# A fused attention and gated-MLP kernel: in block 0, tile 1 turned in two halves around a step of V's first pass, the first half of tile 0's copy cut in two, and tile 2's norm moved behind tile 1's copies

## Chip, cores, metric

One core of one Trainium2 chip. The metric is device time in microseconds (us): the median of several executions. One execution of each kernel is also recorded by the hardware profiler; its span is usually about 1.7 us shorter than the device time (up to about 3 us in single runs). Times like 10.47 below are microseconds from the start of that span.

## The reference, cut

Two rounds of attention (local, dilated, 32 heads) and a gated MLP, each behind a norm, on x of 2048 rows and 1024 columns in bf16:

```python
x = A_x
x = x + _A_ref(_layernorm(x), A_wqkv, A_wo)           # 8 keys per query, 2 apart
x = x + _B_ref(_layernorm(x), W_gate, W_up, W_down)   # relu(gate) * up, then down
# ... the same two lines once more
```

Only the very first step matters here: `_layernorm(x)` of the first 512 rows (block 0, four tiles of 128 rows) and the product of the result with V's weights.

## The kernel before

The opening normalizes tiles 0 to 3, turns each on TensorE (eight 128x128 transposes into PSUM, where TensorE leaves its results), and copies the turned tile to SBUF in two halves. V's first pass is the consumer: for tile 0, four "steps" kc = 0..3 of eight products each, one per chunk of output columns. Step kc reads one eighth of the turned tile and one eighth of the weights. The weights of these steps come in two transfers: rows kc 0 and 1, then rows kc 2 and 3.

```python
def turn(t):
    if t == 0:      # two PSUM tiles, one per half
        tps[t] = [psum.tile([P, KC // 2, P], BF16, tag="acc", name=f"tp{h}")[:] for h in range(2)]
    else:           # one PSUM tile of two banks; each half in a bank of its own
        both = psum_l.tile([P, 2, KC, P], BF16, tag="L", name="tp_pair")
        tps[t] = [both[:, h, 0:KC // 2, :] for h in range(2)]
    for c in range(KC):
        ...         # eight transposes, in order on TensorE

def copy(t, eng, h):
    f = nc.vector.tensor_copy if eng == "v" else nc.scalar.copy
    on(eng, f, hold["xnT"][:, t, h * (KC // 2):(h + 1) * (KC // 2), :], tps[t][h])

scratch(13)                        # 13 products on ones, to warm TensorE up
bn(0, 0); bn(0, 1); aggr(0)        # VectorE: statistics of tile 0
act_square(2); act_mean(2)         # ScalarE: statistics of tile 2
bn(1, 0); apply(0, 0); apply(0, 1)
turn(0); copy(0, "a", 0)           # ScalarE copies the first half of tile 0
bn(1, 1); aggr(1)
copy(0, "v", 1)
act_power(2)
apply(1, 0); apply(1, 1)           # norm of tile 1, in halves, on VectorE

def second():
    turn(1)
    apply(2)                       # norm of tile 2, on VectorE
    copy(1, "v", 0); copy(1, "v", 1)
    act_square(3); act_mean(3); act_power(3); apply(3)
# ... and in V's first pass:
for kc in range(KC // 2):          # KC = 8: four steps for tile 0
    if kc == KC // 2 - 1:
        ln["second"]()             # tile 1 is turned before the fourth step
    for c in range(KC):
        prod(kc, c, 0, 1)
# next on TensorE: 32 products of tile 1, which read the first half of its copy
```

The several instructions of one engine are issued in the order written. Waits between engines are put in by the language, from the tiles that the instructions read and write.

## Time and profile before

| | before |
|---|---|
| device time, median of 3 runs | 1618.47 us (1617.82 to 1618.52) |
| span of the profiled run | 1616.7 us |
| TensorE busy | 1611.1 us |
| first product of V, tile 0 | 7.89 us |
| first product of V, tile 1 | 10.47 us |

Busy times and clock, from the page of the kernel before (busy us, share of the span, instructions; PEclk is the granted clock in tenths, 9 for full, in 40 slices):

```profile
span 1616.7 us, 18929 instructions
PE 1611.1 (100%) x7633; PEld 786.4 (49%) x7633; DVE 1137.4 (70%) x960; ACT 475.5 (29%) x967; POOL 180.9 (11%) x168
PEclk9999999999999999999999999999999999999999
```

TensorE is busy but for 5.6 us, so an edit that leaves its work as it is can gain only where TensorE stands still. The waits of PE, then those of its weight loads for transfers, of the kernel before (total us, times, longest):

```profile
PE scratch L132 <- DVE ones L310: 1.5, 1, 1.5
PE acc_v L132 <- ACT xnT_first L328: 0.6, 1, 0.6
PE acc_v L132 <- DVE xnT_first L106: 0.2, 1, 0.2
```

```profile
PEld L132 <- DMA w_u<-in_B_W_up_dram: 0.6, 1, 0.6
PEld L132 <- DMA w_o<-in_A_wo_dram: 0.5, 1, 0.5
PEld L132 <- DMA w_v<-in_A_wqkv_dram: 0.3, 1, 0.3
```

The first product of V waits 0.6 us for ScalarE's copy, the first product of tile 1 0.2 us for VectorE's. These two waits are what the change is after. The timeline of the kernel before around them (start, duration, engine, line, instruction, then in brackets the engine's idle time and who ended it):

```profile
7.27 0.56 ACT L328 COPY xnT_first<-tp 128x512 bf16<-128x512 bf16 x1
...
7.89 1.51 PE L132 MATMUL acc_v<-xnT_first,w_v 128*128 128x128 bf16 x24 [0.60 <-ACT xnT_first L328]
...
8.63 0.74 DVE L106 TENSOR_SCALAR xn_first<-x,mv,rstd 128x512 bf16<-128x512 bf16 x2 [0.54 <-POOL rstd L328]
...
9.23 0.61 PE L383 MATMUL tp_pair<-ident,xn_first 128*128 128x128 bf16 x8
...
9.54 0.55 DVE L106 TENSOR_SCALAR xn_first<-x,mean,rstd 128x1024 bf16<-128x1024 bf16 x1 [0.17 <-POOL rstd L328]
...
9.68 0.61 PE L132 MATMUL acc_v<-xnT_first,w_v 128*128 128x128 bf16 x8
10.00 0.75 DVE L106 COPY xnT_first<-tp_pair 128x512 bf16<-128x512 bf16 x2
...
10.47 0.72 PE L132 MATMUL acc_v<-xnT_first,w_v 128*128 128x128 bf16 x10 [0.18 <-DVE xnT_first L106]
```

Read it so: 24 products (steps kc 0 to 2), eight transposes of tile 1 (`tp_pair`), the fourth step (9.68), then the products of tile 1 (10.47). VectorE applies tile 2's norm at 9.54, and tile 1's copies follow at 10.00.

### The profile page before, as it was taken

What the parts mean: (1) busy time and instruction counts of PE and PEld (TensorE: products, weight loads), DVE (VectorE), ACT (ScalarE), POOL (GpSimd) and SP (SyncE); (2) the same over time, 40 slices, a digit from 0 to 9 for tenths busy, and PEclk for the clock granted to TensorE, in tenths of its full rate; (3) what the DMA queues carried; (4) which work ended last, traced back from release to release, by engine and by line L of the source; (5) the groups of instructions that cost most, each with busy time, mean ns of one, the idle gap of its engine ahead of it and who ended that gap; (6) DMA issues with size and microseconds to landing.
All of it is one profiled execution on the core that took longest, in us unless ns stands there. A gap on an engine that the chain in (4) does not pass through costs nothing.

```text
span 1616.7 us, 18929 instructions
## 1 busy us (share of the span) xinstructions
PE 1611.1 (100%) x7633; PEld 786.4 (49%) x7633; DVE 1137.4 (70%) x960; ACT 475.5 (29%) x967; POOL 180.9 (11%) x168
## 2 busy tenths in 40 slices
PE   9999999999999999999999999999999999999999
PEld 6646544444444445444454444544445444444444
DVE  5999979996989698929489293893939939311211
ACT  5753312131116313603136031360313311131110
POOL 2400100010003002300053000530005100000000
PEclk9999999999999999999999999999999999999999
DMA  9868868697669766794747947479574884755452
GB/s 302 186 187 242 222 158 261 183 215 204 209 190 220 199 183 213 191 247 149 223 159 204 239 152 228 154 202 256 160 230 153 209 240 156 209 161 177 157 167 67
DMA packets 407448, 317.92 MB, mean 197 GB/s; under 512 B 166464, under 2 KB 387008, under 8 KB 406848
## 3 DMA queue, kind: packets, MB, share of 16 engines
q1 hardware_dynamic: 406784, 316.13, 69.5%
q8 instruction: 59, 0.97, 0.2%
q10 hardware_dynamic: 576, 0.59, 0.1%
q14 instruction: 29, 0.24, 0.0%
HBM read 266.29 MB, written 34.66 MB: 186 GB/s over the span
## 4 chain that ended last, share of the span: by engine, by line
PE 99%; DMA 1%; DVE 0%; POOL 0%; issue 0%; DVEq 0%
PE acc_u L132 24%; PE acc_g L132 24%; PE dacc L132 18%; PE acc_wo L132 7%; PE acc_q L132 7%; PE acc_k L132 7%; PE acc_v L132 7%; PE dacc_pair L132 6%; DMA w_u<-in_B_W_up_dram 0%; DMA x<-in_A_x_dram 0%; POOL rstd L328 0%; DVE xn_first L106 0%; DVE bst L106 0%; PE tp_pair L383 0%; DVE bst L103 0%
## 5 line engine op out<-in xcount | busy, mean ns | idle before, releaser
L132 PE MATMUL acc_u<-xnT_b,w_u 128*128 128x512 bf16 x1792 | 423.3, 379 | 0.1
L132 PE MATMUL acc_g<-xnT_b,w_g 128*128 128x512 bf16 x1792 | 423.3, 379 | 0.0
L784 ACT ACTIVATE r<-acc_g 128x512 bf16<-128x512 f32 x224 | 133.6, 596 | 725.4 <-PE acc_g L132 699.4
L106 DVE TENSOR_TENSOR hT<-acc_u,r 128x512 bf16<-128x512 f32 x224 | 151.3, 690 | 240.6 <-PE acc_u L132 238.2
L132 PE MATMUL dacc<-w_d,hT 128*128 128x512 bf16 (+1 forms) x1400 | 301.9, 375 | 0.0
L132 PEld LDWEIGHTS <-hT 128*128 128x128 bf16 x1820 | 178.1, 98 | 209.0
L132 PEld LDWEIGHTS <-w_u 128*128 128x128 bf16 x1792 | 175.3, 98 | 211.7 <-DMA w_u<-in_B_W_up_dram 0.6
L132 PEld LDWEIGHTS <-w_g 128*128 128x128 bf16 x1792 | 175.3, 98 | 211.4
L106 DVE TENSOR_TENSOR pv<-a,vhm 128x4096 bf16<-128x4096 bf16 x64 | 143.7, 2290 | 0.0
L831 DVE TENSOR_TENSOR x<-dacc,x 128x512 bf16<-128x512 f32 (+1 forms) x38 | 24.5, 673 | 154.1 <-PE dacc L132 154.1
L602 DVE TENSOR_TENSOR t<-q,k 128x2048 f32<-128x2048 bf16 x56 | 128.1, 2293 | 6.7 <-ACT k L537 4.6
L106 DVE TENSOR_TENSOR t<-q,k 128x2048 f32<-128x2048 bf16 x56 | 127.6, 2290 | 3.7 <-ACT k L537 2.6
L106 DVE TENSOR_TENSOR pv<-pv 128x1024 bf16<-128x1024 bf16 (+1 forms) x128 | 113.9, 957 | 0.0
L543 POOL COPY kh<-k 128x14 bf16<-128x14 bf16 x40 | 56.0, 1405 | 504.4 <-ACT k L537 504.4
L132 PE MATMUL acc_wo<-w_o,oT 128*128 128x512 bf16 x512 | 112.0, 379 | 0.0
L615 DVE TENSOR_TENSOR ac<-ac,t 128x2048 f32<-128x2048 f32 x48 | 109.7, 2286 | 0.3
L106 DVE TENSOR_TENSOR ac<-ac,t 128x2048 f32<-128x2048 f32 x48 | 109.8, 2288 | 0.0
L264 POOL TENSOR_TENSOR st_b<-st_b,neg_half 128x1 f32<-128x1 f32 x29 | 43.9, 1521 | 526.2 <-ACT st_b L263 526.2
L132 PE MATMUL dacc_pair<-w_d,hT 128*128 128x512 bf16 x420 | 95.9, 379 | 0.0
L132 PEld LDWEIGHTS <-oT 128*128 128x128 bf16 x512 | 50.1, 98 | 60.6 <-DMA w_o<-in_A_wo_dram 0.5
L259 ACT ACTIVATE xn_b<-x 128x1024 bf16<-128x1024 bf16 x29 | 30.3, 1045 | 128.4 <-DVE x L106 66.3
L441 ACT CAST vT<-acc_v 128x512 bf16<-128x512 f32 x56 | 32.7, 586 | 57.7 <-PE acc_v L132 56.7
(134 smaller groups left out, 1230.1 us busy)
## 6 DMA issues: line engine op xcount, KB each, us to landing
w_g<-in_B_W_gate_dram SPq DMA_DIRECT2D x56, 1024.0 KB, 7.2
w_u<-in_B_W_up_dram SPq DMA_DIRECT2D x56, 1024.0 KB, 5.3
w_d<-in_B_W_down_dram SPq DMA_DIRECT2D x48, 1024.0 KB, 5.7
w_o<-in_A_wo_dram SPq DMA_DIRECT2D x16, 1024.0 KB, 7.1
vhm<-v_d SPq DMA_DIRECT2D x32, 284.0 KB, 6.8
v_d<-vT SPq DMA_DIRECT2D x8, 1024.0 KB, 9.6
oT<-o_d SPq DMA_DIRECT2D x32, 256.0 KB, 4.0
w_d<-in_B_W_down_dram SPq DMA_DIRECT2D x16, 512.0 KB, 3.8
```

What stands on the lines that cost most here:

```text
L106: tail_dve[0] = f(*args, **kwargs).ins
L132: tail_pe[0] = nc.tensor.matmul(*args, **kwargs).ins
L259: nc.scalar.activation(xn, xt[:], ACT.Square, accum_out=sq)
L264: nc.gpsimd.tensor_tensor(rstd, vpe, neg_half[:, 0:1], op=ALU.pow)
L441: tail_act[0] = nc.scalar.copy(st["vT"][:, c, :], acc[:]).ins
L543: nc.gpsimd.tensor_copy(khalo[n][:, c, :], k[:, BLK:BLK + HALO])
L602: nc.vector.tensor_tensor(t[:], i0, i1, op=ALU.mult)
L615: nc.vector.tensor_tensor(o, ac[:], t[:], op=ALU.add)
L784: tail_act[0] = nc.scalar.activation(rs[j][:], acc[:], ACT.Relu).ins
L831: run = dv if n < NB - 2 else (lambda f, *args, **kwargs: f(*args, **kwargs))
```

## The change

The intent: let V start when a quarter of tile 0 is copied (ScalarE's half is copied in two quarters, VectorE's half stays whole); turn only the first half of tile 1 before the fourth step, so that its copy runs under that step; and let tile 1's copies go ahead of tile 2's norm on VectorE.

```diff
-        def turn(t):
-            if t == 0:
+        def turn(t, halves=(0, 1)):
+            if t in tps:
+                pass
+            elif t == 0:
 ...
-            for c in range(KC):
+            for c in (h * (KC // 2) + i for h in halves for i in range(KC // 2)):
 ...
-        def copy(t, eng, h):
+        def copy(t, eng, h, i0=0, i1=KC // 2):
 ...
-        copy(0, "a", 0)
+        copy(0, "a", 0, 0, KC // 4)
+        copy(0, "a", 0, KC // 4, KC // 2)
 ...
-        def second():
-            turn(1)
+        def second(h):
+            turn(1, (h,))
+            if h == 0:
+                copy(1, "v", 0)
+                return
+            copy(1, "v", 1)
             apply(2)
-            copy(1, "v", 0)
-            copy(1, "v", 1)
             act_square(3)
 ...
                 if kc == KC // 2 - 1:
-                    ln["second"]()
+                    ln["second"](0)
                 for c in range(KC):
                     prod(kc, c, 0, 1)
+            ln["second"](1)
```

More of the change, by code (lines that the diff above doesn't have):

```diff
@@ L384, in turn @@
                                                      xna[:, t, c * P:(c + 1) * P], ident[:]).ins
-        def copy(t, eng, h):
+        def copy(t, eng, h, i0=0, i1=KC // 2):
             f = nc.vector.tensor_copy if eng == "v" else nc.scalar.copy
-            on(eng, f, hold["xnT"][:, t, h * (KC // 2):(h + 1) * (KC // 2), :], tps[t][h])
+            on(eng, f, hold["xnT"][:, t, h * (KC // 2) + i0:h * (KC // 2) + i1, :], tps[t][h][:, i0:i1, :])
         warm = small("warm")
```

## The prediction

> **What bounds the kernel now.** TensorE: busy 1611.1 of 1616.7 us (the page's busy times), 99% of the chain of waits, clock 1.0. After the opening 10.5 us only two weight loads wait visibly (w_u 0.6 us, w_o 0.5 us). So the change can win only in the opening, where the waits of PE list 0.60 us at 7.89 (first product waits for ScalarE's copy of tile 0) and 0.18 us at 10.47 (first product of tile 1 waits for VectorE's copy; 0.34 us of issue time).
>
> **The three parts, read from the timeline.**
> 1. *Quartered copy.* ScalarE takes 1.057 us for 1024 columns and 0.565 for 512, so I estimate 0.32 for 256: the first products could start at about 7.64, not 7.89. But the third step's weights are the second w_v transfer, which lands at 8.73; its weight load starts at 8.774 already now. Sixteen products at 56 ns (the Trainium skill, "TensorE: Matmul & The Clock Gate", section "Wait — 56ns, not 53.3ns?", gives the same 56) end at 8.53 and then wait about 0.25 us for that DMA. The wait only moves; worth about 0.
> 2. *Norm of tile 2 later.* Its 0.55 us on VectorE (9.54 to 10.09) now delays tile 1's first copy (10.00). Moved, it costs nothing: its reader, the turn of tile 2, starts at 14.0.
> 3. *Tile 1 in halves.* Four transposes at 9.23, step 4 from 9.46 to 9.90, four more transposes. The first copy can start at about 9.67 and end at 10.08. PE's work is contiguous to 10.13, so tile 1's products could start then: 0.34 us earlier. However both halves share one PSUM tile, and the trace shows dependencies kept for whole tiles: ScalarE's copy of tile 3 waits for all eight transposes (17.735), VectorE's copy of the other half waits for ScalarE's (18.353), the additions of dacc_pair wait for both halves (708.77). The Trainium skill, "PSUM — Partial Sum Buffer", section "PSUM bank collisions raise a hardware error", says different banks run clean, so this is the program's own caution. If it also holds writer after reader, the last four transposes wait for the copy (about 10.13), end at 10.36, and the gain is only 0.11 us. I think this more likely.
>
> **On the critical path.** 0.1 to 0.35 us in all, carried to the end because later DMA issues follow PE's releases; w_v's last rows (landed 12.107, wanted 12.474) leave room. The added ScalarE copy (0.3 us) falls on an engine idle until 9.43. The spread of the three runs is 0.7 us, larger than the gain.
>
> **Predicted:** 1618.3 us, 8 in 10 between 1617.4 and 1619.0. Faster by over 2%: 0.003; within 2%: 0.994; slower: 0.003.
>
> **What would show each step.** Right: first w_v product near 7.64; a new wait for w_v of about 0.25 us ending near 8.77; VectorE's tile-1 copy near 9.67; PE waiting 0.2 us for that copy before the second four transposes, or no wait (then 0.34 us gained); first tile-1 product at 10.13 to 10.36; everything later shifted by that amount. Wrong: the third step starts before 8.7, or tile 1's products start at 10.47 or later.
>
> **What would make it wrong.** The w_v transfer landing earlier (then part 1 counts, up to 0.25 us); the split turn making PE wait longer; an instruction order changed far from the edit, moving the two later DMA waits; drift between runs larger than the effect.

## The result

| | before | after |
|---|---|---|
| device time, median of 5 runs | 1618.47 us (1617.82 to 1618.78) | 1618.19 us (1618.10 to 1618.90) |
| span of the profiled run | 1616.7 us | 1616.4 us |
| second half of x tile 0 landed | 3.78 | 4.20 |
| second w_v transfer landed | 8.73 | 8.11 |
| first product of V, tile 0 | 7.89 | 8.09 |
| first product of V, tile 1 | 10.47 | 10.64 |

The ratio of after to before is 0.9999, with a 95% interval of 0.9986 to 1.0013: the same. (A ratio is the mean time of one kernel's fast runs over the mean of the other's fast runs of the same rounds, so it is not quite the ratio of the medians.)

The same lines of the kernel after: busy times, waits of PE (its weight loads now wait for no transfer at all), timeline:

```profile
span 1616.4 us, 18930 instructions
PE 1611.3 (100%) x7633; PEld 786.6 (49%) x7633; DVE 1137.1 (70%) x960; ACT 475.8 (29%) x968; POOL 180.4 (11%) x168
```

```profile
PE scratch L132 <- DVE ones L310: 1.5, 1, 1.5
PE acc_v L132 <- ACT xnT_first L328: 0.4, 1, 0.4
```

```profile
7.68 0.63 ACT L328 COPY xnT_first<-tp 128x256 bf16<-128x256 bf16 x2
...
8.09 1.50 PE L132 MATMUL acc_v<-xnT_first,w_v 128*128 128x128 bf16 x24 [0.40 <-ACT xnT_first L328]
...
9.04 0.74 DVE L106 TENSOR_SCALAR xn_first<-x,mv,rstd 128x512 bf16<-128x512 bf16 x2 [0.54 <-POOL rstd L328]
...
9.51 0.40 PE L385 MATMUL tp_pair<-ident,xn_first 128*128 128x128 bf16 x4
...
9.74 0.61 PE L132 MATMUL acc_v<-xnT_first,w_v 128*128 128x128 bf16 x8
...
9.94 0.42 DVE L106 COPY xnT_first<-tp_pair 128x512 bf16<-128x512 bf16 x1 [0.17 <-PE tp_pair L385]
...
10.42 0.38 PE L385 MATMUL tp_pair<-ident,xn_first 128*128 128x128 bf16 x4
...
10.64 0.55 PE L132 MATMUL acc_v<-xnT_first,w_v 128*128 128x128 bf16 x7
```

The new order is there, and the second four transposes wait for the copy: they start at 10.42, just after its end at 10.37 (9.94 + 0.42, before rounding). But the opening of this run is *later* than before: x arrived about 0.4 us later (ScalarE's copy starts at 7.68 against 7.27), and tile 1's products start 0.17 us later. Nevertheless the span is 0.28 us shorter.

Setting every TensorE instruction after the opening against its counterpart shows where that comes from. The kernel after is 0.167 us late from 10.64 to 160 us. It loses the whole lag at one weight load of w_o, for which before waited (160.93), and gets ahead to 0.268 us at one weight load of w_u, for which before waited too (247.54). After that the distance stays at 0.27 to 0.28 us to the end. So in this pair of profiles all of the visible gain comes from two waits far from the edit. The question for the experiments is whether the edit removed them, and what the edit is worth in the opening once the arrival of x is accounted for.

### The profile page after: what moved, and what is told of

Same layout as the page of the kernel before. It is cut to its first block, busy times and chain, and to the rows that moved or that the text cites. A ratio compares the mean times of both kernels' runs of the same rounds, so it can differ in the third digit from the quotient of the medians.

```text
span 1616.4 us, 18930 instructions
## 1 busy us (share of the span) xinstructions
PE 1611.3 (100%) x7633; PEld 786.6 (49%) x7633; DVE 1137.1 (70%) x960; ACT 475.8 (29%) x968; POOL 180.4 (11%) x168
## 4 chain that ended last, share of the span: by engine, by line
PE 99%; DMA 0%; ACT 0%; DVE 0%; issue 0%; ACTq 0%; DVEq 0%
PE acc_u L132 24%; PE acc_g L132 24%; PE dacc L132 18%; PE acc_v L132 7%; PE acc_wo L132 7%; PE acc_k L132 7%; PE acc_q L132 7%; PE dacc_pair L132 6%; DMA x<-in_A_x_dram 0%; ACT xn_first L328 0%; PE tp_pair L385 0%; PE L L132 0%; DVE x L837 0%; DVE xnT_first L106 0%; ACTq L175 0%
```

## The experiments

Theory: the edit is worth a tenth or two of a microsecond in the opening; the waits on w_o and w_u are chance. Rival: the edit removes these waits, and the opening depends on luck alone. Every kernel was built from one of the two, gave the correct result, and was timed for five rounds against the kernel before. Each of the eleven ratios was between 0.9998 and 1.0002 with intervals within 0.9985 to 1.0015.

The expectations use M, from the landing of the second half of x tile 0 to tile 1's first product. M turned out to be a poor measure: the opening depends on other arrivals too. The table therefore has the gates in their order. T is the start of tile 1's turn, Q the start of tile 1's first product.

| profile | x tile 2 landed | first product | second w_v landed | third step | half 1 of tile 1's norm ends | T | Q | Q - T | span - Q |
|---|---|---|---|---|---|---|---|---|---|
| before | 5.01 | 7.89 | 8.73 | 8.78 | 9.05 | 9.23 | 10.47 | 1.236 | 1606.18 |
| after | 5.42 | 8.09 | 8.11 | 8.98 | 9.45 | 9.51 | 10.64 | 1.131 | 1605.74 |
| control_before | 5.14 | 8.08 | 8.72 | 8.97 | 9.01 | 9.41 | 10.54 | 1.125 | 1605.74 |
| control_after | 5.00 | 7.66 | 8.74 | 8.79 | 9.01 | 9.24 | 10.37 | 1.122 | 1605.77 |
| quarters_only | 4.94 | 7.62 | 8.18 | 8.51 | 8.91 | 8.97 | 10.34 | 1.373 | 1605.81 |
| move_only | 5.02 | 7.90 | 7.99 | 8.79 | 9.00 | 9.23 | 10.36 | 1.125 | 1605.74 |
| no_quarters | 5.26 | 8.13 | 8.72 | 9.03 | 9.02 | 9.47 | 10.59 | 1.122 | 1605.78 |
| quarters_move | 5.32 | 8.12 | 8.01 | 9.01 | 9.01 | 9.46 | 10.59 | 1.126 | 1606.28 |
| norm_in_front | 5.15 | 7.82 | 8.51 | 8.71 | 9.00 | 9.15 | 10.65 | 1.493 | 1606.16 |
| two_tiles | 5.04 | 7.70 | 8.92 | 8.97 | 9.01 | 9.42 | 10.32 | 0.902 | 1605.90 |
| two_tiles_again | 5.61 | 8.46 | 9.72 | 9.77 | 9.60 | 10.23 | 11.13 | 0.902 | 1606.21 |
| copy_first | 4.88 | 7.58 | 8.83 | 8.87 | 8.92 | 9.33 | 10.45 | 1.122 | 1605.74 |
| two_tiles_copy_first | 4.93 | 8.27 | 9.51 | 9.56 | 8.84 | 10.02 | 10.91 | 0.900 | 1605.78 |

Two columns do the work. Q - T belongs to the program and hardly to the arrivals: runs of one order agree within 0.01 us, save for the kernel before, where it also depends on whether tile 2's norm is out of the way in time (1.236 and 1.125). Span - Q is 1605.74 to 1605.81 us in eight profiles of thirteen and up to 0.5 us more in the others.

### control_before: the kernel before again

> The kernel before, unchanged, profiled again. Measure M: from the landing of the second half of x tile 0 to the start of the first product of tile 1 (6.69 us in the first profile: 3.78 to 10.47). If the opening follows the arrival of x, as I think, M is 6.69 within 0.05 whatever the landing. If the two stalls of the first profile (acc_wo at 160.93, 0.49 us of idle weight load; acc_u at 247.54, 0.59 us) are chance of the DMA, at least one is missing or over 0.1 us different here; the rival, that they belong to the kernel before and that the change removed them, expects both again and a span of 1616.7 against 1616.4 to 1616.6 of the kernel after.

Measured: 1618.00 us median; M is 6.84, so the expectation on M was missed. The wait on w_o is gone and the one on w_u is 0.2 us instead of 0.6. The span is 1616.3, shorter than every span of the kernel after in its first rounds (1616.4 to 1616.6). The rival falls: here the kernel before lacks the one wait and has a third of the other, and kernels with the change have them (two_tiles_again waits 0.8 us for w_o, norm_in_front 0.7 us for w_u). control_after itself waits 0.4 us for w_u. They are chance as far as this edit goes: set instruction by instruction, the kernel after against the one before and the other ten profiles against copy_first, the distance after the opening changes by more than 0.04 us only at these two weight loads, together by up to 0.5 us of span (last column). What decides when these weights land is not shown.

The waits of weight loads for w_u in control_before and in control_after, then that for w_o in two_tiles_again (total us, times, longest):

```profile
PEld L132 <- DMA w_u<-in_B_W_up_dram: 0.2, 1, 0.2
...
PEld L132 <- DMA w_u<-in_B_W_up_dram: 0.4, 1, 0.4
...
PEld L132 <- DMA w_o<-in_A_wo_dram: 0.8, 1, 0.8
```

### control_after: the kernel after again

> The kernel after, unchanged, profiled again. M was 6.44 us (4.20 to 10.64). My theory, that the edit is worth 0.25 us in the opening and the rest of the 0.28 us of span is chance, expects M 6.44 within 0.05 whatever the landing of x, unless the second w_v transfer lands late (then up to 0.1 more). The rival, that M depends on luck of the transfers and not on the edit, expects M to overlap that of the kernel before.

Measured: 1618.16 us median; M is 6.64, missed by 0.2, because the second w_v transfer landed at 8.74. This is the case that the prediction described. Its timeline:

```profile
7.26 0.63 ACT L328 COPY xnT_first<-tp 128x256 bf16<-128x256 bf16 x2
...
7.66 1.75 PE L132 MATMUL acc_v<-xnT_first,w_v 128*128 128x128 bf16 x24 [0.40 <-ACT xnT_first L328]
...
8.78 0.45 PEld L132 LDWEIGHTS <-w_v 128*128 128x128 bf16 x8 [0.24 <-DMA w_v<-in_A_wqkv_dram]
...
9.24 0.39 PE L385 MATMUL tp_pair<-ident,xn_first 128*128 128x128 bf16 x4
...
9.47 0.61 PE L132 MATMUL acc_v<-xnT_first,w_v 128*128 128x128 bf16 x8
9.67 0.42 DVE L106 COPY xnT_first<-tp_pair 128x512 bf16<-128x512 bf16 x1 [0.34 <-PE tp_pair L385]
...
10.15 0.38 PE L385 MATMUL tp_pair<-ident,xn_first 128*128 128x128 bf16 x4
...
10.37 0.83 PE L132 MATMUL acc_v<-xnT_first,w_v 128*128 128x128 bf16 x12
```

The first product is at 7.66 instead of 7.89, and the head start is lost again in a wait of 0.24 us for w_v. From there to tile 1's products everything is within 0.02 us of the numbers predicted. Against the first profile of before, whose third step started at the same time (8.78 and 8.79), tile 1's first product is 0.104 us earlier. So the edit has a worth of its own in these two profiles; how it depends on the arrivals is worked out below.

### quarters_only

```diff
  # from the kernel after; some lines are joined here
-            turn(1, (h,))
-            if h == 0: copy(1, "v", 0); return
-            copy(1, "v", 1)
-            apply(2)
+            if h == 1: return
+            turn(1)
+            apply(2)
+            copy(1, "v", 0); copy(1, "v", 1)
```

> Only the quartered copy of tile 0; tile 1 turned whole, tile 2's norm ahead of the copies as before. My theory: the first product comes 0.2 us earlier from the landing (3.89 against 4.11 us), but M stays 6.69 within 0.05, because the second four transposes wait for the second half of tile 1's norm (about 5.6 us after the landing) and the copy waits behind tile 2's norm. The rival, that the quartered copy carries the gain by itself, expects M near 6.47.

Measured: 1618.03 us median; M is 6.71, as expected, though the first product came only 0.11 us earlier from the landing (3.995), not 0.2. w_v was early here, and the third step started at 8.51, the earliest of all. That lead did not come through:

```profile
8.97 0.72 PE L385 MATMUL tp_pair<-ident,xn_first 128*128 128x128 bf16 x8
9.41 0.55 DVE L106 TENSOR_SCALAR xn_first<-x,mean,rstd 128x1024 bf16<-128x1024 bf16 x1 [0.18 <-POOL rstd L328]
...
9.87 0.75 DVE L106 COPY xnT_first<-tp_pair 128x512 bf16<-128x512 bf16 x2
...
10.34 0.44 PE L132 MATMUL acc_v<-xnT_first,w_v 128*128 128x128 bf16 x5 [0.21 <-DVE xnT_first L106]
```

The transposes took 0.72 us instead of 0.61, because the second four waited for the second half of tile 1's norm. Their results were there before 9.7, but tile 2's norm held VectorE until 9.95. Q - T is 1.373, the second worst. In this profile the quarters gave nothing, because tile 1's copy stood behind tile 2's norm, and the quarters do not move that norm. It is no rule: in control_before that copy waited for the last transpose instead, and there quarters would have been worth about 0.08 us even with the norm in front (an estimate by the arithmetic near the end).

### move_only

```diff
  # from the kernel before: only the order on VectorE
             turn(1)
-            apply(2)
             copy(1, "v", 0)
             copy(1, "v", 1)
+            apply(2)
```

> Only tile 2's norm moved behind tile 1's copies; tile 1 turned whole, tile 0 copied in one piece by ScalarE. My theory: the first copy no longer waits for the norm but for all eight transposes of its tile, so M is about 6.58 (0.11 less than before). The rival, that the move alone gives nothing without the halves, expects M 6.69; that it gives all, 6.44.

Measured: 1618.45 us median; M is 6.64 (expected 6.58), and Q - T is 1.125 against 1.236 before, with T at 9.23 in both:

```profile
9.23 0.61 PE L385 MATMUL tp_pair<-ident,xn_first 128*128 128x128 bf16 x8
...
9.88 0.76 DVE L106 COPY xnT_first<-tp_pair 128x512 bf16<-128x512 bf16 x2 [0.56 <-PE tp_pair L385]
```

The copy now waits for the eighth transpose and for nothing else. These 0.11 us are the whole gain of control_after over before (Q - T of 1.122). The move alone carries it. In control_before T was late (9.41), the norm was done when the last transpose was, and the kernel before had 1.125 as well: there the move would be worth nothing. T was late because ScalarE's copy waited for tile 0's transposes, which started at 7.02 instead of 6.57, right behind the last warm-up product (started at 6.62, and these were still 0.427 us apart; quarters_move shows the same).

### no_quarters and quarters_move

no_quarters is the kernel after with `copy(0, "a", 0)` whole; quarters_move is the kernel after with tile 1 turned whole (`turn(1)`, both copies, then `apply(2)`).

> The kernel after without the quartered copy: halves and moved norm only. My theory: the three first steps end 0.1 us later than the first half of tile 1's norm allows, so M is about 6.54 to 6.58, 0.10 to 0.14 above the kernel after. The rival, that the quarters are worth nothing because their head start is lost in later waits (as I predicted for a late w_v), expects M 6.44.

> The kernel after with tile 1 turned whole (quarters and moved norm kept). My theory: the second four transposes wait for the second half of tile 1's norm, the first copy for all eight transposes, so M is about 6.40 to 6.58: the halves then are worth between -0.04 and 0.14 us. The rival, that the split turn is the main term, expects M 6.69.

Measured: 1618.50 and 1618.59 us median; M is 6.87 and 6.85, both far outside what was expected, because x tile 2 came about 0.3 us later than in control_after (5.26 and 5.32 against 5.00), and with it ScalarE's copy (7.52 and, held up by tile 0's transposes as well, 7.70 against 7.26). On M they decide nothing. On Q - T they do: 1.122 with halves and 1.126 without, at equal T (9.47 and 9.46). The split turn is worth 0.004 us there. In the first profile of after it was worth more: T waited for the first half of tile 1's norm (9.45), and a whole turn would have waited for the second half (9.77). That is worth about 0.1 us, an estimate from these two ends; no run isolates it. Nor does any run isolate the quarters with the move in place. In no_quarters the second w_v transfer (8.72) was there before the third step, which started 0.89 us after the first product; a copy of 0.35 us instead of 0.565 would have brought all of it about 0.21 us forward. That is an estimate from these durations.

### norm_in_front

```diff
  # from the kernel after
             if h == 0:
+                apply(2)
                 copy(1, "v", 0)
                 return
             copy(1, "v", 1)
-            apply(2)
```

> The kernel after with tile 2's norm put back in front of tile 1's first copy (halves and quarters kept). My theory: the norm cannot start before its rstd (about 5.7 us after the landing), the copy follows it, and the second four transposes and tile 1's products wait for that copy, so M is about 6.85, worse than before. The rival, that the norm's place hardly matters, expects M 6.44.

Measured: 1618.49 us median; M is 6.94 (expected 6.85) and Q - T 1.493, the worst of all:

```profile
9.15 0.39 PE L385 MATMUL tp_pair<-ident,xn_first 128*128 128x128 bf16 x4
...
9.49 0.55 DVE L106 TENSOR_SCALAR xn_first<-x,mean,rstd 128x1024 bf16<-128x1024 bf16 x1 [0.17 <-POOL rstd L328]
...
9.96 0.42 DVE L106 COPY xnT_first<-tp_pair 128x512 bf16<-128x512 bf16 x1
...
10.43 0.38 PE L385 MATMUL tp_pair<-ident,xn_first 128*128 128x128 bf16 x4 [0.44 <-DVE xnT_first L106]
```

With halves but without the move, TensorE itself waits: the second four transposes stand behind the copy, and the copy behind the norm. The halves need the move.

### two_tiles: two PSUM tiles for tile 1

```diff
  # from the kernel after
-            elif t == 0:
+            elif t <= 1:
                 tps[t] = [psum.tile([P, KC // 2, P], BF16, tag="acc", name=f"tp{h}")[:] for h in range(2)]
```

> The kernel after with the two halves of tile 1 turned into two separate PSUM tiles, as tile 0's are. My theory, that the second four transposes wait for VectorE's copy only because both halves are one tile to the program's dependencies, expects no wait of PE between the eight products of step 4 and the second four transposes, and M about 6.22, that is 0.22 less than the kernel after, span about 1616.2. The rival, that the wait has another cause (the norm of tile 1, or the bank itself), expects M 6.44 with the wait still there.

Measured: 1618.12 us median. M is 6.61, not 6.22, since the second w_v transfer was late (8.92). The wait, however, is gone, and Q - T is 0.902, 0.22 us less than in control_after:

```profile
9.42 0.39 PE L385 MATMUL tp<-ident,xn_first 128*128 128x128 bf16 x4
...
9.65 0.61 PE L132 MATMUL acc_v<-xnT_first,w_v 128*128 128x128 bf16 x8
9.85 0.42 DVE L106 COPY xnT_first<-tp 128x512 bf16<-128x512 bf16 x1 [0.51 <-PE tp L385]
...
10.09 0.39 PE L385 MATMUL tp<-ident,xn_first 128*128 128x128 bf16 x4
...
10.32 0.89 PE L132 MATMUL acc_v<-xnT_first,w_v 128*128 128x128 bf16 x13
```

The second transposes start at 10.09, right after the fourth step and in the middle of the copy (9.85 to 10.27). In both kernels the halves lie in different banks by the program's layout (no trace shows addresses); what differs is that they are two tiles, which here come from another pool of PSUM as well. In all five profiles with split halves in one tile the second transposes start 0.05 us after the end of the copy, and norm_in_front's line names that copy. So the wait in the kernel after (0.23 us of issue time in control_after, from the end of the fourth step's issue at 9.92 to 10.15) is the program's own, between a reader and a later writer of one tile.

### copy_first, two_tiles_copy_first, two_tiles_again

In all profiles so far ScalarE's first copy started 2.25 us or more after x *tile 2* had landed, because its two passes over tile 2 stand ahead of it. These runs take one of the passes out of the way.

```diff
  # from the kernel after, and from two_tiles
         act_square(2)
-        act_mean(2)
 ...
         copy(0, "a", 0, KC // 4, KC // 2)
+        act_mean(2)
 ...
-        act_power(2)
         apply(1, 0)
         apply(1, 1)
+        act_power(2)
```

> The kernel after with ScalarE's quartered copy of tile 0 put ahead of its mean of tile 2 (and tile 2's variance behind tile 1's norm). In the nine runs so far but one the copy started 2.25 to 2.27 us after x tile 2 landed, whatever tile 0 did, or just after tile 0's transposes when these were later. My theory: the copy now starts about 0.05 us after the fourth transpose of tile 0 ends, before x tile 2's landing plus 2.2 us. The gain ends at the next gate: the third step starts at the later of 0.89 us after the first product and 0.046 us after the second w_v transfer lands; tile 1's turn at the later of 0.457 us after the third step and 0.055 us after the first half of tile 1's norm (about 9.06); tile 1's first product 1.12 us after its turn starts. With the second w_v transfer landing near 8.73 that is 10.36, as in the kernel after; with 8.0 to 8.2 it is about 10.2. The rival, that the copy waits for tile 0's transposes and not for tile 2, expects its start unmoved at x tile 2's landing plus 2.26 us.

> Both: two PSUM tiles for tile 1 and ScalarE's copy ahead of its mean of tile 2. My theory: tile 1's first product 0.90 us after its turn starts, that is at 9.96 to 10.15 by the landing of the second w_v transfer, 0.2 us ahead of the kernel after at equal landings; span 1605.74 us plus that, plus 0 to 0.5 us of chance in the weight waits at 160 and 247 us; by the clock still the same, far inside 2%.

> The two-tile kernel unchanged, profiled again: from the start of tile 1's turn to its first product 0.90 us within 0.02, as before (the kernel after: 1.12 to 1.13), whatever the landings. The rival, that the first run was luck, expects 1.0 or more. The weight waits at 160 and 247 us differ from the first run's if they are chance.

(The first text says "but one"; two of the ten profiles are later than 2.27: control_before 2.30 and quarters_move 2.38.) Measured: 1618.02, 1618.15 and 1618.13 us median. In copy_first the copy starts 1.99 us after tile 2's landing, released by tile 0's transposes:

```profile
6.88 0.65 ACT L328 COPY xnT_first<-tp 128x256 bf16<-128x256 bf16 x2 [0.82 <-PE tp L385]
...
7.57 0.17 PEld L132 LDWEIGHTS <-w_v 128*128 128x128 bf16 x3 [0.59 <-DMA w_v<-in_A_wqkv_dram]
```

The next gate is the *first* w_v transfer, which the expectation had left out; then the second one, at 8.83. Tile 1's first product was expected at 10.45 for that landing (8.83 + 0.046 + 0.457 + 1.12) and came at 10.45. In two_tiles_copy_first both transfers landed later than in all others but two_tiles_again (8.22 and 9.51), and the expected 9.96 to 10.15 was missed: 10.91, which is what its own landing gives (9.51 + 0.046 + 0.457 + 0.90). Q - T was 0.900, and 0.902 in two_tiles_again, so the two-tile gain repeats. By the clock no version beats the two kernels: two_tiles_again has a ratio of 0.9999 (0.9986 to 1.0011), copy_first 0.9998.

## Why the prediction was right, and where it was not

The time was predicted as 1618.3 us and measured as 1618.19; "within 2%" had a chance of 0.994. The number alone shows little: a forecast of no change (1618.47) lies in the stated range of 1617.4 to 1619.0 too, and in the profiled pair the predicted sign and size came from two chance waits, as the second point shows. That was luck. The reasons, point by point:

- **"The change can win only in the opening"**: shown. Span minus Q is 1605.74 to 1605.81 us in eight profiles of thirteen, whatever Q was (10.34 to 10.91), and the other five lose their 0.1 to 0.5 us at w_o and w_u. A shift in the opening passes to the end one for one; only the waits on w_o and w_u add to it, by chance.
- **"Everything later shifted by that amount"** was wrong for the pair compared: the two chance waits of before are larger than the effect and turned a lag of 0.17 us into a lead of 0.28 us.
- **Quartered copy, "the wait only moves; worth about 0"**: the mechanism was seen in control_after (first product 7.66, predicted 7.64; wait of 0.24 us for w_v, predicted 0.25). But it took one landing for a fixed one. The second w_v transfer landed between 7.99 and 8.92 in the first ten profiles, and 8.11 in the first profile of after. There the third step did not wait for w_v at all, and "worth about 0" fails: with a whole copy everything up to the third step would have been 0.21 us later, and tile 1's first product about 0.14 us (estimates from the copies' durations and the gates below; the rest is hidden by tile 1's norm). The prediction had named an early w_v as what would make it wrong. Its sign for that, a third step before 8.7, did not show (8.98), because x was late.
- **Halves: "the gain is only 0.11 us"**: the size was right for arrivals as in the first profile, the part was not. With the quarters above, this is the step that failed. move_only has 0.111 us of it without any halves, and the halves add 0.003 (1.125 to 1.122) with T at the same place. The prediction had rightly seen that the norm delays the copy (10.00), but said of the move only that it costs nothing, and booked the gain under the halves.
- **"If it also holds writer after reader, the last four transposes wait for the copy"**: shown by two_tiles, which removes that wait and 0.22 us; 0.23 us had been predicted (0.34 less 0.11). The Trainium skill, "PSUM — Partial Sum Buffer", section "PSUM bank collisions raise a hardware error", says that accesses to different banks run clean; two_tiles agrees: transposes at 10.09 into one bank, a copy until 10.27 out of another (banks by the program's layout), result correct.
- **"First tile-1 product at 10.13 to 10.36"**: 10.64 in the profile of after, past the 10.47 that the prediction called wrong; 10.37 in control_after. An absolute time was a bad test, since x arrived 0.4 us later in that run.

What is the edit worth? The gates of the table reproduce the opening: the first product 0.05 us after the copy (or 0.046 after the first w_v transfer); the third step at the later of 0.89 us after the first product and 0.046 after the second w_v transfer; T at the later of 0.457 us after the third step and 0.055 after the norm's first half; Q from T by the kernel's order. This arithmetic, with durations from the traces and each profile's own start of ScalarE's copy, gives Q within 0.03 us in the first ten profiles. Run for both orders on the arrivals of each of the ten, it gives the change a worth of 0.00 to 0.26 us, about 0.17 in the mean. Added one after the other, the move gives about 0.04 of that mean, the quarters 0.10 (0 to 0.21; nothing where w_v is the last to come, as in control_after), and the halves 0.03. So the part that the prediction wrote off may be the largest. These are estimates, not measurements: 0.01% of the time, where five runs of one kernel spread over 0.4 to 1.6 us. What stays open is why the transfers land as differently as they do.

## What to carry to other kernels

When an edit is worth a fraction of a microsecond, compare intervals between two instructions that the same program fixes, not absolute times or spans: here Q - T of the two-tile order repeated to 0.002 us while the transfer that gates it moved by 0.8 us. When several reorderings come together, run each alone, and each with the others in place: the plain one (a norm moved behind a copy) carried the 0.11 us that had been credited to the clever one (the split turn), and what the quarters add to the move is still only an estimate, because no run isolates it. If two halves of a buffer shall be filled and emptied by different engines at once, give them two tiles, because waits may be kept for the whole tile even where the hardware would not need them.

## What the Trainium skill lacked or had wrong

- "DMA: Bandwidth & Descriptors" gives a fit for the duration of one transfer (measured for transfers that GpSimd issues; the w_v ones are issued by SyncE), but no section says how far it varies between executions of one program. Here the second 512 KB w_v transfer, issued at 2.20 us in the first profiles and within 0.01 us of that in all, landed between 7.99 and 9.72 us in thirteen profiles, and x tile 0's second half between 3.56 and 4.33. That is more than the whole edit is worth.
- "TensorE: Matmul & The Clock Gate", section "What you observe", puts the change to the fast clock around 4 us into sustained activity, 500 ns more or less. The 13 warm-up products start at 1.52 us, 0.427 us apart while cold. They went fast after 3.4 us in two_tiles_again and were still slow at the last one, 5.1 us after the first, in the first profile of after. The spread seen is wider than the page's figure there, though the page's own note that the same kernel shows different counts of slow products fits.
- The same page, section "Wait — 56ns, not 53.3ns?", agrees: 56 ns between products of 128 columns in the opening.
- "PSUM — Partial Sum Buffer" tells what the hardware allows by bank, but no page tells that the program's waits may be kept for a whole PSUM tile of two banks. It cost 0.22 us here (1.122 against 0.902).
